# Tiles of x, of its sums and of the dense activations moved to 64 bytes off a multiple of 128

## The chip, the cores and the metric

One Trainium2 chip, one of its cores. The metric is device time in microseconds (us) of one launch. PE is TensorE, with PEld for its weight loads; DVE is VectorE, ACT ScalarE, POOL GpSimd, SP SyncE.

## What is computed

Three layers in a row on 1152 tokens of width 512, all in float32:

```python
scores = scale * q @ k.T + min(-(cum_i - cum_j), 0)   # causal, 2 x 8 heads, 576 x 64
x = softmax(scores) @ v                               # -> (1152, 512)
p = domain_probs / domain_probs.sum(-1)               # 4 experts
x = sum_e p[:, e] * (relu(x @ w1[e]) @ w2[e])         # w1 512 x 1024, w2 1024 x 512
out = (silu(x @ w_gate) * (x @ w_val)) @ w_out        # 512 x 1536, 1536 x 512
```

## The kernel before

A small planner inside the kernel (`Plan`) decides, with a table of costs and ranks, on which engine each step runs and in which order. It does so while the program is built, so the order on each engine is fixed then. The change touches none of its numbers.

**Exact products from parts.** Every operand of a dense matmul is held as a high part and a low part (`xh`/`xl` for x, `wah`/`wal`, `wsh`/`wsl` and `woh`/`wol` for weights, `hh`/`hl` for the activations between two matrices), and each product is three matmuls: high by high, high by low, low by high. Each matmul is one weight load of 128 by 128 (PEld) and one stream of 256, 320 or 512 columns (PE). The operand that streams is called moving here, the one that is loaded is called stationary.

**Into the hidden layer.** `into` (lines 1040 to 1042) does it plainly for the first five weights. After that `seven` (lines 1144 to 1146) does a block of 2 by 2 quarters with seven products instead of eight, from sums of quarters of the weight (`wsh`, `wsl`) and sums of quarters of x (tiles `xh0`, `xl0` for tokens 0 to 511, `xh512`, `xl512` for tokens 512 to 1151). In both, x or its sums are moving and the weight is stationary. The columns are 256 for the first half of the tokens and 320 for the second; one product is six matmuls. The table of the seven products, as (weight part, x part), says which tiles each one reads; a pair means the operand itself, a single number one of its sums:

```python
SEVEN = [((0, 0), (0, 0)), ((0, 1), (1, 0)), (0, 1), (2, 0), (1, 2), (3, (1, 1)), ((1, 1), 3)]
```

So products 0 and 1 read x itself with `wah`/`wal`; products 2, 3 and 4 read sums of x with `wsh`/`wsl`; product 5 reads x itself with `wsh`/`wsl`; product 6 reads sums of x with `wah`/`wal`. The trace leaves the numbers off tile names: `xh` there stands for `xh`, `xh0` and `xh512`, and the product tells which it is.

**Out of the hidden layer.** `outof` (lines 1202 to 1204): the activations `hh`, `hl` are stationary, the weights `woh`, `wol` are moving, 512 columns, three matmuls per block of 128 tokens and 128 hidden units. Results are taken from PSUM by DVE (line 1316, with the gate `pr`; line 1464 in the last layer).

**Order.** `merge` puts the `outof` work of one stage behind three quarters of the `seven` work of the next. A stage then reads: products 0 to 4 in one run of 30 matmuls, 3 matmuls of `outof`, product 5 (6 matmuls), some `outof`, product 6 (6 matmuls), the rest of `outof`.

**Where tiles lie.** A pool hands out its tiles one behind the other; each takes a multiple of 32 bytes of every partition. The pool `const` is at the bottom of SBUF, and the pool `tm` (opened when attention is done, line 1593) takes the space that attention leaves. The starts of the tiles, in bytes modulo 128, in the built programs:

| tiles | before | changed |
|---|---|---|
| `xh`, `xl` (x itself), `acc_a` | 0 | 64 |
| `xh0`, `xl0` (sums, first half) | 64 | 64 |
| `xh512`, `xl512` (sums, second half), `acc_b` | 0 | 64 |
| `hh`, `hl` in `tm`; also `cc`, `tt`, `x32`, `sg` | 0 | 64 |
| `hh`, `hl` in `hA` (first stages, and one weight in three of the last layer) | 0 | 0 |
| `wah`, `wal`, `wsh`, `wsl`, `woh`, `wol`, `raw`, `sf` | 0 | 0 |

All slices that a dense matmul reads start a multiple of 128 bytes into their tile, so the row of a tile holds for each of its matmuls. `xh0` and `xl0` lie at 64 before the change because the small tiles ahead of them in `const` (`pr` with 160 bytes, `warm` with 32) add up so.

Of the kernel before, what the change touches and what calls it, by code (L numbers as in the profile page):

```python
# [9 lines left out]
F32 = mybir.dt.float32  # L10
# [8 lines left out]
P = 128  # L19
# [3 lines left out]
HALF = 512  # L23
PIECES = 2
PLAIN = 5
NS = 5
NKQ = 8
NKP = 2
# [81 lines left out]
def dve(c, n=1):  # L110
    return n * 0.07 + 0.00105 * c
# [53 lines left out]
class Plan:  # L165
# [8 lines left out]
    def add(self, eng, cost, run=None, deps=(), take=(), give=(), rank=0.0, port="p", mode="r"):  # L174
        t = Task(eng, cost, run, [d for d in deps if d is not None], take, give, rank, port, mode)
        if not t.missing:
            self.ready.append(t)
        return t
# [102 lines left out]
def attention_moe_swiglu(ctx, tc, q_early, q_late, k, v, s, dp, w1, w2, wg, wv, wo, out):  # L281
# [4 lines left out]
    NT, _, DM = out.shape  # L286
    N = NT * P
    E = dp.shape[2]
# [15 lines left out]
    const = ctx.enter_context(tc.tile_pool(name="const", bufs=1))  # L304
# [2 lines left out]
    psw = ctx.enter_context(tc.tile_pool(name="psw", bufs=1, space=PSUM))  # L307

    ident = const.tile([P, P], F32, name="ident")
    xh = const.tile([P, NC, N], F32R, name="xh")  # L310
    xl = const.tile([P, NC, N], F32R, name="xl")
    acc_a = const.tile([P, HALF // P, DM], F32, name="acc_a")
    pr = const.tile([P, NT, E], F32, name="pr")
    late = {}
    plan = Plan()
    add = plan.add
    rings = {}
# [1 line left out]
    def ring(name, n=2):  # L319
        return rings.setdefault(name, Ring(n))  # L320
# [36 lines left out]
    def attention(ap, ps):  # L357
# [162 lines left out]
        def inorder(stage, t):  # L520
            before[stage] = t
            return t

        def group(i, pi, ch, qbs):
# [42 lines left out]
            def least(x, lane, at, w):  # L567
                def run():
                    if "st" not in box:
                        box["st"] = next(stats)  # L570
                    if lane not in box["ns"]:
                        box["ns"][lane] = ap.tile([P, S], F32, name="ns", tag="ns", bufs=NS)
                    st, ns = box["st"][:, 2 * x:2 * x + 2], box["ns"][lane]
                    if two:
                        todo = [(s0, s1, y[:, :s1 - s0], decay[pi, 2][:, s0:s1]) for y, (s0, s1) in zip(box["sp"], spans)]
                    else:
                        todo = [(at, at + w, box["sp"][lane][:, at:at + w], mask[:, 2 * P - w:] if pi < EXACT else decay[pi][:, lane, :w])]
                    for y, (s0, s1, sp, bias) in enumerate(todo):
                        nc.vector.tensor_tensor_reduce(
                            ns[:, s0:s1], sp, bias, SC, st[:, 0:1] if y else 3.0e38, op0=ALU.add, op1=ALU.min, accum_out=st[:, y:y + 1])  # L580
                return run
# [33 lines left out]
            for x, lane, (qb, at, w) in todo:  # L615
                new, final = lane not in owner, x == L - 1
                tM = inorder("m", add("dve", dve(w, len(spans)) + 0.01, least(x, lane, at, w), [tS if pi or lane else ready[-1], before.get("m")] + bias,
                                      take=[ring("ns", NS)] if new else [], give=[(tS, rg)] + (used[pi] if qbs[-1] == ch.qbs[-1] else [])
                                      if final else [], rank=i + x + RANK["m"]))
# [345 lines left out]
    narrow = [[Narrow(w[u]) for w in (wg, wv, wo)] for u in wide]  # L965
    halves_n = iter([(x, a) for u in narrow for x in u for a in range(2)])
    late["narrowed"] = []
    late["warm"] = const.tile([P, 1], F32, name="warm")
    w_in = [Weight(w1[i], False, "wa") for i in range(n1)]
    for w in w_in[PLAIN:]:  # L970
        w.plain = False
# [503 lines left out]
    def jobs():  # L1475
# [16 lines left out]
        late["pace"] = 2 * n1 - len(part) + sum(t1 < HALF for t1 in part) - CALM - REST  # L1492
        assert len(part) == PLAIN, len(part)
        for t0, t1 in ((0, HALF), (HALF, N)):
# [73 lines left out]
    def feed():  # L1568

        while sum(t.end is None for t in open_pe) < 6:  # L1570
            open_pe[:] = [t for t in open_pe if t.end is None]
            if not next(work, False):
                return
# [17 lines left out]
    with ExitStack() as st:  # L1591
        late["ps"] = st.enter_context(tc.tile_pool(name="psb", bufs=1, space=PSUM, reuse_waits="tile"))
        late["t"] = st.enter_context(tc.tile_pool(name="tm", bufs=2, reuse_waits="tile"))
        late["h"] = late["t"]
        late["acc"] = late["t"].tile([P, NT - HALF // P, DM], F32, name="acc_b", bufs=1)
        late["T", HALF] = {x: late["t"].tile([P, 4, 2, (N - HALF) // 2], F32R, name=f"x{x}{HALF}", bufs=1) for x in "hl"}
        sums_of_x(HALF)
        add("act", 1.3, lambda: nc.scalar.activation(late["warm"], late["warm"], AF.Silu), [late["gates"]], rank=0)
        late["made_n"] = 0
        plan.held, plan.ported = HELD2, False  # L1600
        rings["h"].n, rings["o"].n = 5, 3
        feed()
        while plan.step():
            feed()
# [70 lines left out]
```

## Time and profile before

| | us |
|---|---|
| median of 3 runs (697.23 to 697.93) | 697.86 |
| the profiled execution, its own time | 697.67 |
| its span, first to last instruction | 695.9 |
| PE busy in the span | 686.0 |
| DVE, POOL, ACT busy | 533.2, 461.8, 361.9 |

The span leaves 1.8 us of the execution's own time outside it. Rows of groups carry the busy time of one kind of instruction and its mean duration; matmuls are pipelined, so the duration of one (some 390 ns for 512 columns) is longer than its share of the engine. That share is the distance from the start of one matmul to the start of the next, which the rows in order of time show.

### The profile page before, as it was taken

Reading aid. Unit: us, or ns where it says so; the run is one execution under the profiler, and the core shown is the slowest. Engines: PE = TensorE matmul, PEld = TensorE weight load, DVE = VectorE, ACT = ScalarE, POOL = GpSimd, SP = SyncE. Lnnn points to the kernel's source line nnn. Section 1 sums busy time; section 2 is a strip of 40 time slices with the busy share of each in tenths; the row PEclk is TensorE's granted clock in tenths of the full one; section 3 lists DMA queues with packets and bytes.
Section 4 is the critical chain, followed back from the end, with each engine's and each line's share of the span. In section 5 each row is a group of like instructions: output and inputs, shape, how many; then the busy total and the mean of one; then the engine's idle time right before and its main releaser. Section 6 shows DMA issues by size and latency. Waiting matters only on the chain.

```text
span 695.9 us, 11938 instructions
## 1 busy us (share of the span) xinstructions
PE 686.0 (99%) x4267; PEld 600.4 (86%) x4267; DVE 533.2 (77%) x1086; ACT 361.9 (52%) x763; POOL 461.8 (66%) x464
## 2 busy tenths in 40 slices
PE   8999999999999999999999899999999999999998
PEld 6766667889898989898989799898999999999996
DVE  7866756795588999989988988786865766676665
ACT  7978777344655555554655654356555332323110
POOL 2888746786665776586667667598996838383211
PEclk9999999999999999999999999999999999999999
DMA  6786451120334455554653453213021111000003
GB/s 199 259 287 207 153 161 31 43 80 32 122 122 151 137 171 178 158 165 163 195 172 120 151 197 122 77 36 98 19 91 61 62 31 63 30 31 1 1 1 136
DMA packets 30187, 78.45 MB, mean 113 GB/s; under 512 B 3488, under 2 KB 8096, under 8 KB 30128
## 3 DMA queue, kind: packets, MB, share of 16 engines
q1 hardware_dynamic: 29984, 77.56, 34.2%
q8 instruction: 33, 0.54, 0.3%
q14 instruction: 26, 0.21, 0.1%
q10 hardware_dynamic: 144, 0.13, 0.1%
HBM read 65.85 MB, written 11.83 MB: 112 GB/s over the span
## 4 chain that ended last, share of the span: by engine, by line
PE 88%; DVE 4%; ACT 4%; DMA 2%; issue 1%; POOL 1%; SPq 0%; DVEq 0%; ACTq 0%; POOLq 0%
PE h L1146 13%; PE h L1145 13%; PE h L1144 13%; PE o L1202 13%; PE o L1203 12%; PE o L1204 12%; PE po L698 2%; PE tp L639 2%; ACT ns L588 2%; PE sp L557 2%; PE h L1040 1%; PE h L1042 1%; PE h L1041 1%; DMA d<-rows 1%; ACT ns L335 1%
## 5 line engine op out<-in xcount | busy, mean ns | idle before, releaser
L1163 DVE TENSOR_TENSOR cc<-cc,h 128x320 f32<-128x320 f32 (+1 forms) x306 | 137.0, 453 | 73.1 <-PE h L1146 62.0
L1202 PE MATMUL o<-woh,hh 128*128 128x512 f32 x398 | 157.6, 396 | 2.1 <-DVE xl L1355 1.1
L1203 PE MATMUL o<-wol,hh 128*128 128x512 f32 x398 | 155.6, 391 | 0.0
L1204 PE MATMUL o<-woh,hl 128*128 128x512 f32 x398 | 154.8, 389 | 0.0
L1144 PE MATMUL h<-xh,wsh 128*128 128x320 f32 (+1 forms) x344 | 101.7, 296 | 0.0
L1145 PE MATMUL h<-xl,wsh 128*128 128x320 f32 (+1 forms) x344 | 101.6, 295 | 0.0
L1146 PE MATMUL h<-xh,wsl 128*128 128x320 f32 (+1 forms) x344 | 101.6, 295 | 0.0
L1285 ACT ACTIVATE cc<-cc 128x640 f32<-128x640 f32 (+1 forms) x54 | 37.5, 695 | 104.3 <-DVE cc L1163 104.1
L340 POOL TENSOR_TENSOR wal<-raw,wah 128x512 fp32r<-128x512 f32 (+1 forms) x58 | 68.3, 1189 | 35.2 <-ACT wah L327 34.3
L1204 PEld LDWEIGHTS o<-woh,hl 128*128 128x128 f32 x398 | 74.8, 188 | 16.6 <-DVE hl L340 0.5
L1202 PEld LDWEIGHTS o<-woh,hh 128*128 128x128 f32 x398 | 74.8, 188 | 14.8 <-issue 1.3
L340 POOL TENSOR_TENSOR hl<-cc,hh 128x512 fp32r<-128x512 f32 (+1 forms) x28 | 41.9, 1495 | 68.1 <-ACT hh L1288 64.7
L340 POOL TENSOR_TENSOR wol<-raw,woh 128x512 fp32r<-128x512 f32 x54 | 75.8, 1419 | 13.2 <-ACT woh L327 12.4
L1203 PEld LDWEIGHTS o<-wol,hh 128*128 128x128 f32 x398 | 74.9, 188 | 9.9
L1146 PE MATMUL h<-xh,wal 128*128 128x320 f32 (+1 forms) x258 | 76.6, 297 | 0.0
L1145 PE MATMUL h<-xl,wah 128*128 128x320 f32 (+1 forms) x258 | 76.5, 297 | 0.0
L1144 PE MATMUL h<-xh,wah 128*128 128x320 f32 (+1 forms) x258 | 76.4, 296 | 0.0
L340 POOL TENSOR_TENSOR wsl<-sf,wsh 128x512 fp32r<-128x512 f32 x48 | 68.2, 1439 | 2.6 <-ACT wsh L327 2.5
L1144 PEld LDWEIGHTS h<-xh,wsh 128*128 128x128 f32 x344 | 64.7, 188 | 1.7
L1145 PEld LDWEIGHTS h<-xl,wsh 128*128 128x128 f32 x344 | 64.7, 188 | 1.6
L1146 PEld LDWEIGHTS h<-xh,wsl 128*128 128x128 f32 x344 | 64.7, 188 | 0.0
L1316 DVE SCALAR_TENSOR_TENSOR acc_b<-o,pr,acc_b 128x512 f32<-128x512 f32 x75 | 55.2, 742 | 5.6 <-PE o L1204 5.4
(158 smaller groups left out, 1557.4 us busy)
## 6 DMA issues: line engine op xcount, KB each, us to landing
raw<-in_w SPq DMA_DIRECT2D x42, 512.0 KB, 5.0
n<-hl SPq DMA_DIRECT2D x36, 256.0 KB, 2.4
raw<-n SPq DMA_DIRECT2D x18, 512.0 KB, 3.3
hh<-in_wg SPq DMA_DIRECT2D x12, 512.0 KB, 3.8
hh<-in_wv SPq DMA_DIRECT2D x12, 512.0 KB, 4.2
hh<-in_wo SPq DMA_DIRECT2D x12, 512.0 KB, 4.0
dql<-rows SPq DMA_DIRECT2D x8, 512.0 KB, 4.7
vr<-in_v SPq DMA_DIRECT2D x4, 640.0 KB, 4.5
```

What stands on the lines that cost most here:

```text
L340: {"v": nc.vector, "p": nc.gpsimd}[e].tensor_tensor(to, x, f32(y), op=ALU.subtract)
L557: nc.tensor.matmul(sp[j][:, at:at + w], Q[half[j], x], K[half[j], :w], start=True, stop=False)
L588: nc.scalar.activation(ns, ns, AF.Exp, bias=st[:, y:y + 1], scale=-1.0, accum_out=st[:, 8 + x:9 + x])
L1144: nc.tensor.matmul(hp, wh, h, start=c == 0, stop=False)
L1145: nc.tensor.matmul(hp, wh, l, start=False, stop=False)
L1146: nc.tensor.matmul(hp, wl, h, start=False, stop=c == 1)
L1163: nc.vector.tensor_tensor(part(k), part(x), banks[i], op=ALU.add)
L1202: nc.tensor.matmul(op, hh[:, f, ts], wh[:, f, y], start=f == 0, stop=False)
L1203: nc.tensor.matmul(op, hh[:, f, ts], wl[:, f, y], start=False, stop=False)
L1204: nc.tensor.matmul(op, hl[:, f, ts], wh[:, f, y], start=False, stop=f == NF - 1)
L1285: nc.scalar.activation(src()[:, o], src()[:, o], AF.Relu)
L1316: nc.vector.scalar_tensor_tensor(acc(t), bank_(), sc, acc(t), op0=ALU.mult, op1=ALU.add)
```

## The change

`pr` and `warm` are allocated ahead of `xh`, `xl` and `acc_a` instead of behind them, which moves those three by 192 bytes and leaves what follows where it was. In the pool `tm` a tile `line` of 64 bytes, which nothing reads or writes, comes first and moves every later tile of that pool by 64 bytes.

```diff
+LINE = 16
@@
     ident = const.tile([P, P], F32, name="ident")
+    pr = const.tile([P, NT, E], F32, name="pr")
+    late = {"warm": const.tile([P, 1], F32, name="warm")}
+
     xh = const.tile([P, NC, N], F32R, name="xh")
     xl = const.tile([P, NC, N], F32R, name="xl")
     acc_a = const.tile([P, HALF // P, DM], F32, name="acc_a")
-    pr = const.tile([P, NT, E], F32, name="pr")
-    late = {}
@@
-    late["warm"] = const.tile([P, 1], F32, name="warm")
@@
         late["h"] = late["t"]
+        late["t"].tile([P, LINE], F32, name="line", bufs=1)
         late["acc"] = late["t"].tile([P, NT - HALF // P, DM], F32, name="acc_b", bufs=1)
```

The lists of instructions of all engines are the same before and after, in the same order with the same shapes; only addresses differ.

## Rows read from the trace of the kernel before

**Rows 1.** Span and mean granted TensorE clock; then the page's busy time of the engines.
```profile
core 0: 695.9 us, clock 1.000
...
PE 686.0 (99%) x4267; PEld 600.4 (86%) x4267; DVE 533.2 (77%) x1086; ACT 361.9 (52%) x763; POOL 461.8 (66%) x464
```

**Rows 2.** The page: chain of work that ended last, by engine.
```profile
PE 88%; DVE 4%; ACT 4%; DMA 2%; issue 1%; POOL 1%; SPq 0%; DVEq 0%; ACTq 0%; POOLq 0%
```

**Rows 3.** Groups by shape, PE: first of the three lines of each product.
```profile
L1202 PE MATMUL o<-woh,hh 128*128 128x512 f32 x394 | 156.5, 397 | 2.1 <-DVE xl L1355 1.1 <-DVE acc_a L1316 1.0
...
L1144 PE MATMUL h<-xh,wsh 128*128 128x320 f32 x192 | 59.4, 309 | 0.0
...
L1144 PE MATMUL h<-xh,wah 128*128 128x320 f32 x144 | 44.4, 308 | 0.0
L1144 PE MATMUL h<-xh,wsh 128*128 128x256 f32 x152 | 42.4, 279 | 0.0
...
L1144 PE MATMUL h<-xh,wah 128*128 128x256 f32 x114 | 32.0, 281 | 0.0
L1040 PE MATMUL h<-xh,wah 128*128 128x256 f32 x48 | 14.0, 292 | 0.0
...
L1144 PE MATMUL h<-xh,hl 128*128 128x320 f32 x32 | 9.9, 308 | 0.0
...
L1144 PE MATMUL h<-xh,hh 128*128 128x320 f32 x24 | 7.4, 308 | 0.0
```

**Rows 4.** Order of time, PE, one stage of 256 columns: products 0 to 4.
```profile
296.26 0.28 PE L1146 MATMUL h<-xh,wal 128*128 128x256 f32 x1
...
297.46 0.29 PE L1144 MATMUL h<-xh,wsh 128*128 128x256 f32 x1
...
297.82 0.28 PE L1144 MATMUL h<-xh,wsh 128*128 128x256 f32 x1
...
299.52 0.39 PE L1202 MATMUL o<-woh,hh 128*128 128x512 f32 x1
```

**Rows 5.** The same stage: product 5, between two runs of `outof`.
```profile
299.75 0.40 PE L1203 MATMUL o<-wol,hh 128*128 128x512 f32 x1
299.99 0.39 PE L1204 MATMUL o<-woh,hl 128*128 128x512 f32 x1
300.22 0.28 PE L1144 MATMUL h<-xh,wsh 128*128 128x256 f32 x1
300.33 0.28 PE L1145 MATMUL h<-xl,wsh 128*128 128x256 f32 x1
...
300.93 0.40 PE L1202 MATMUL o<-woh,hh 128*128 128x512 f32 x1
```

**Rows 6.** Order of time, PE, a stage of 320 columns: products 2 to 4.
```profile
423.07 0.31 PE L1144 MATMUL h<-xh,wsh 128*128 128x320 f32 x1
...
425.71 0.39 PE L1202 MATMUL o<-woh,hh 128*128 128x512 f32 x1
```

**Rows 7.** Order of time, PE: a longer run of `outof`, 512 columns.
```profile
301.63 0.40 PE L1202 MATMUL o<-woh,hh 128*128 128x512 f32 x1
...
304.13 0.39 PE L1204 MATMUL o<-woh,hl 128*128 128x512 f32 x1
```

**Rows 8.** Order of time, PE: product 6 behind a run of `outof`.
```profile
305.04 0.28 PE L1144 MATMUL h<-xh,wah 128*128 128x256 f32 x1
...
305.74 0.39 PE L1202 MATMUL o<-woh,hh 128*128 128x512 f32 x1
```

**Rows 9.** Windows of 40 us: PE, PEld, DVE, ACT, POOL busy (count), clock, DMA, GB/s.
```profile
220.00:260.00 40.00, 40.00 (x235) 35.74 (x234) 37.43 (x60) 22.55 (x40) 28.78 (x23) 1.00 0.45 152
...
460.00:500.00 40.00, 39.95 (x254) 36.34 (x254) 30.73 (x57) 23.07 (x51) 37.80 (x41) 1.00 0.16 53
```

**Rows 10.** Groups by shape, ACT: casts of 256 columns.
```profile
L327 ACT CAST wah<-raw 128x256 fp32r<-128x256 f32 x19 | 7.7, 405 | 13.1 <-PE h L1145 12.9
...
L327 ACT CAST xh<-sf 128x256 fp32r<-128x256 f32 x7 | 2.8, 399 | 1.2 <-POOL sf L1082 1.2
```

## The prediction

> **What bounds the kernel now.** I read the page first: PE is busy 686.0 of 695.9 us at a granted clock of 1.000, and no other engine is above 77% [rows 1]. The chain that ended last agrees: 88% of it is PE [rows 2]. So the end is set by how fast PE gets through its list, above all in the dense part, from about 130 us on. There a busy share of 99% tells nothing, since matmuls overlap; I looked at the distance from start to start instead.
>
> At the granted clock of 1.00, the upper of the two levels (2.4 GHz), one column per cycle, 256, 320 and 512 columns need 106.7, 133.3 and 213.3 ns. The rows show more. A run of `outof` takes 2.50 us for 11 matmuls, 227.3 ns each [rows 7]: 14.0 over. The 18 matmuls of 320 columns take 2.64 us, 146.7 ns each [rows 6]: 13.4 over. So each matmul carries a surcharge that does not depend on its columns, as a cost of its weight load would.
>
> One stage of the kernel before holds the experiment already. Products 0 and 1 read x itself, at 0 modulo 128: the last ten of their twelve matmuls take 1.20 us, 120.0 ns each. Products 2 to 4 have the same shape and read the sums of x, which lie at 64: after three slower ones (0.36 us), the last fifteen take 1.70 us, 113.3 ns each [rows 4]. The stationary tile differs as well (`wah` there, `wsh` here), but product 5 tells these apart: it loads `wsh` and streams x itself, and from its second matmul on it takes 0.60 us for five, 120.0 ns each [rows 5]. So it goes with where the moving tile lies: 13.3 ns of surcharge with both operands at 0, 6.7 ns with 64 between them. The reading I take is that the stream and the weight load running beside it get in each other's way in SBUF, less so when they start in different halves of 128 bytes.
>
> The Trainium skill speaks against this reading: "TensorE: Matmul & The Clock Gate", Part 2, step 1, says that PE has two independent read ports into SBUF, so that loading the next weights takes no bandwidth from the running matmul. By that rule tile starts would not matter; the 120.0 beside 113.3 ns disagrees, and the rule gets a rival below.
>
> **The change, part by part.** No instruction is added, removed or moved. All costs come from addresses.
>
> *Streams that gain.* 320 columns: the groups have 192 + 144 per line, and two smaller ones (32 + 24) where the weight sits in `hA`, times three lines, 1176 matmuls [rows 3]. All of them go from 0/0 to 64/0. At 6.7 ns this is 7.9 us. 256 columns in `seven`: 152 + 114, and again 32 + 24, times three, 966; three products of seven read x itself, 414, and the rest lies at 64 already. With the 48 times three of `into` [rows 3] 558 gain: 3.7 us. 512 columns: 394 times three, 1182 [rows 3], less 84 early ones (counted in the program's list) whose activations lie in `hA` and stay at 0: 1098, at 6.7 ns 7.4 us. Here it is the stationary operand that moves. No row shows a stationary tile at 64 under a moving one at 0. Its price lies between nothing (only the moving start counts) and 6.7 ns (only the difference counts). I take 6.7, because the surcharge at 0/0 is nearly the same for all three lengths (13.3, 13.4, 14.0) and so looks like one cause with two equal partners. Together 19.0 us, the ceiling.
>
> *What switches take back.* PE changes between x and `outof` 131 times each way (counted in the list); most runs of x are of 6 or 30 matmuls, those of `outof` of 3 to 18. Around a switch the gain is not there. Product 6, six matmuls that already read at 64, takes 0.70 us behind `outof` [rows 8]; product 5, at 0, takes 0.71 [rows 5]. So six matmuls behind a switch gain about nothing, 40 ns a time. Some 110 of the 131 runs of x are among those counted above: 4.4 us. The first three of `outof` behind sums at 64 take 0.70 us, from 299.52 to 300.22 [rows 4, 5], against 0.68 in the steady run [rows 7]; I let them gain nothing either: 132 runs by 3 by 6.7 ns, 2.6 us. That leaves 12.0 us.
>
> A price of the skill's, for comparison: the same page, Part 1, gives a back-to-back matmul as its columns over the clock plus about 2.5 ns. Were that reached, the saving per matmul would be about 11 ns instead of 6.7, and the ceiling an estimated 31 us; the 113.3 ns at 64 show that this offset does not get there.
>
> *What reaches the end.* 12.0 us over some 560 us of dense work is 0.86 us in 40. The fullest neighbours are DVE, 37.43 of 40 us from 220 to 260, and POOL, 37.80 from 460 to 500 [rows 9]. Both have over 2 us left, more than 0.86. So neither becomes the bound, but queues get tighter and PE will meet a late operand more often. I take off a tenth: 10.8 us.
>
> *Other engines.* They read and write the moved tiles as well. The one clean pair is an ACT cast of 256 columns: 405 ns from 0 to 0, 399 ns into the sums at 64 [rows 10]. I put them at nothing: PE's work covers theirs as long as they keep the idle time of those windows [rows 9]. If DVE's operations became 2% longer, its fullest window would still fit in 40 us.
>
> **Sum.** 697.67 us of the profiled execution less 10.8 is 686.9; the median of the runs is 0.19 higher, so I forecast 687.1.
>
> **Rivals.**
> 1. *Nothing happens* (7%): the ports are independent and 113.3 comes from something else that goes with the sums, such as their being written by other engines. Against it stands product 5, which changes only the moving tile. Time 697.9.
> 2. *Only the moving start counts* (22%): the 512s keep 227 ns, since the weights stay at 0. For it: every row at 64 is one of a moving tile. The gain is (7.9 + 3.7 - 4.4) by 0.9, 6.5 us: 691.4.
> 3. *Only the 256s gain* (5%): at 320 and 512 columns the weight load ends well ahead of the stream, and the surcharge there has another cause. Against it: the equal surcharge. 3.7 us, less about half at switches: 696.0.
> 4. *No loss at switches* (10%): with all activations moved too, the pieces behind a switch settle at once; the whole ceiling reaches the end: 678.9.
> 5. *`outof` gets worse* (4%), the other side: a stationary tile at 64 under a stream from 0 does not settle, and each of the 1098 takes the 0.24 us that one matmul behind a switch shows, 299.75 to 299.99 [rows 5], instead of 0.227. That is 13 ns by 1098, 14 us, against the 6.5 us that x gains: 705.4. It decides from 6 ns more per matmul of `outof`, 233 ns, on.
>
> **How the numbers follow.** My own case has 52%; within it, losses at switches between none on `outof` and twice what I took put the time between 682 and 691. About 0.2%, 1.4 us, can be told from no change here. Faster by more than that: 52 + 22 + 5 + 10 = 89%. The same: 7%. Slower: 4%. The range leaves out rival 1, rival 5, rival 3 and about half of rival 4, some 20%: 680.0 to 695.0.
>
> **What would show it.** In the changed profile: products 0 and 1 at 256 columns at 113 ns from start to start in the run, 320 columns at 140, `outof` at 220 in its longer runs; six-long runs behind a switch near 0.70 us at 256 columns; the same durations on ACT and DVE; less idle time of DVE in the window from 220 us on. Wrong would be: 147 ns at 320 columns (rival 3 or 1), 227 at 512 (rival 2), over 233 (rival 5), or the spacings as forecast with new idle time on PE that keeps the end where it was (then my tenth was too little).

## The result and the profile after

The changed kernel takes 701.76 us (median of 4 runs, 701.03 to 701.91), the kernel before 697.89 beside it (4 runs). The ratio is 1.0053, with a 95% interval of 1.0035 to 1.0070: 3.9 us slower by the medians, where 10.8 us faster, 687.1, was forecast. The profiled execution has a span of 700.1 us, 4.2 more than [rows 1].

The page of the changed kernel, its engines:

```profile
span 700.1 us, 11938 instructions
...
PE 690.3 (99%) x4267; PEld 599.6 (86%) x4267; DVE 531.3 (76%) x1086; ACT 362.1 (52%) x763; POOL 462.0 (66%) x464
```

PE is busy 4.3 us longer, and DVE, ACT and POOL as long as before to within 2 us. So the time went into the matmuls themselves and not into waits, nor into more work of the other engines.

The changed kernel's groups by shape on PE (one of the three lines for 256 and 320 columns; lines lie one or two further down than before):

```profile
L1203 PE MATMUL o<-woh,hh 128*128 128x512 f32 x394 | 157.6, 400 | 2.1 <-DVE xl L1356 1.0 <-DVE acc_a L1317 1.0
L1205 PE MATMUL o<-woh,hl 128*128 128x512 f32 x394 | 155.8, 395 | 0.0
L1204 PE MATMUL o<-wol,hh 128*128 128x512 f32 x394 | 155.5, 395 | 0.0
L1145 PE MATMUL h<-xh,wsh 128*128 128x320 f32 x192 | 59.3, 309 | 0.0
...
L1145 PE MATMUL h<-xh,wah 128*128 128x256 f32 x114 | 31.8, 279 | 0.0
```

Beside [rows 3]: `outof` went from 397 to 400 ns on its first line, 320 columns stayed at 309, and the group of products 0, 1 and 6 at 256 columns fell from 281 to 279. The order of time shows what that is from start to start. PE, the same stage of 256 columns as [rows 4, 5, 7] (rows between those shown are left out):

```profile
298.54 0.28 PE L1145 MATMUL h<-xh,wah 128*128 128x256 f32 x1
...
301.27 0.39 PE L1203 MATMUL o<-woh,hh 128*128 128x512 f32 x1
...
301.96 0.28 PE L1145 MATMUL h<-xh,wsh 128*128 128x256 f32 x1
...
302.66 0.39 PE L1203 MATMUL o<-woh,hh 128*128 128x512 f32 x1
...
303.35 0.39 PE L1203 MATMUL o<-woh,hh 128*128 128x512 f32 x1
...
306.62 0.39 PE L1205 MATMUL o<-woh,hl 128*128 128x512 f32 x1
```

From 298.54 to 301.27 stand 24 matmuls, the last 6 of x itself and 18 of its sums, 113.8 ns each: here x itself goes as fast as its sums, where it took 120.0 ns in [rows 4]. Product 5 takes 0.70 us, as forecast. But the run of `outof` takes 3.27 us for 14 matmuls, 233.6 ns each, against 227.3 in [rows 7]. And a run of 320 columns has not moved: 18 matmuls in 2.64 us, 146.7 ns each, as in [rows 6].

```profile
425.58 0.31 PE L1145 MATMUL h<-xh,wsh 128*128 128x320 f32 x1
...
428.22 0.39 PE L1203 MATMUL o<-woh,hh 128*128 128x512 f32 x1
```

The surcharge of a matmul is the time from its start to the next start, less its columns at the granted 2.4 GHz. Added up over all dense matmuls of each trace (the 2% of gaps with over 40 ns of surcharge are left out):

| surcharge | matmuls | before, us (mean ns) | changed, us (mean ns) |
|---|---|---|---|
| `outof`, 512 columns | 1136 | 17.7 (15.6) | 22.1 (19.5) |
| x itself, 256 columns | 545 | 6.7 (12.3) | 5.4 (9.8) |
| sums of x, 256 columns | 548 | 4.7 (8.7) | 5.1 (9.4) |
| 320 columns | 1171 | 15.3 (13.1) | 15.4 (13.1) |
| all, with some 50 others | | 45.3 | 48.8 |

That is 3.5 of the 4.2 us. The "others" are mainly matmuls of `into` with 512 columns, which stream x and which the prediction did not count: they too got slower, from 16.0 to 20.0 ns. The missing 0.7 us is there by 37 us into the matmuls, in attention, before most dense work; its cause is not shown, and it may be the spread of single executions (696.5 to 700.9 for the kernel before in later comparisons).

### The profile page after: what moved, and what is told of

Read it like the earlier page. It is cut to its first block, busy times and chain, and to the rows that moved or that the text cites. A ratio compares the mean times of both kernels' runs of the same rounds, so it can differ in the third digit from the quotient of the medians.

```text
span 700.1 us, 11938 instructions
## 1 busy us (share of the span) xinstructions
PE 690.3 (99%) x4267; PEld 599.6 (86%) x4267; DVE 531.3 (76%) x1086; ACT 362.1 (52%) x763; POOL 462.0 (66%) x464
## 4 chain that ended last, share of the span: by engine, by line
PE 83%; DVE 4%; POOL 4%; ACT 3%; DMA 3%; issue 2%; SPq 1%; POOLq 0%; ACTq 0%; DVEq 0%
PE h L1145 13%; PE h L1146 13%; PE h L1147 13%; PE o L1203 12%; PE o L1205 12%; PE o L1204 12%; ACT ns L590 2%; PE po L700 1%; DMA d<-rows 1%; PE tp L641 1%; POOL sf L1083 1%; PE h L1041 1%; PE h L1043 1%; PE h L1042 1%; DMA raw<-in_w 1%
## 5 line engine op out<-in xcount | busy, mean ns | idle before, releaser
L1205 PE MATMUL o<-woh,hl 128*128 128x512 f32 x398 | 156.9, 394 | 0.0
L342 POOL TENSOR_TENSOR wol<-raw,woh 128x512 fp32r<-128x512 f32 x54 | 75.8, 1419 | 13.5 <-ACT woh L329 12.7
```

Source lines behind the costliest of these rows:

```text
L342: {"v": nc.vector, "p": nc.gpsimd}[e].tensor_tensor(to, x, f32(y), op=ALU.subtract)
L1205: nc.tensor.matmul(op, hl[:, f, ts], wh[:, f, y], start=False, stop=f == NF - 1)
```

## The experiments

Twelve kernels were run. The first four, timed together, take the change apart and move other tiles instead. "Distance" is the start of the stationary tile less that of the moving one; starts are those of the built programs.

**x alone.** The first half of the change's diff (`pr` and `warm` ahead of `xh`) without `line`.

> Only x itself and acc_a move to 64; sums of the second half and the activations stay at 0. If the loss of the change comes from outof alone, products that read x itself at 256 columns go from 120 ns to 113 to 117 ns, 320 columns stay at 147, outof at 227, and the time falls by 558 x 3 ns, 1.6 us, to 696.3. If moving x is what costs (rival: later data for PE, other engines slower on moved tiles), the time is 698 to 702.

It took 698.19 us, ratio 0.9998 (0.9986 to 1.0011): no difference. The trace tells why. x itself gains 1.2 us (12.3 to 10.2 ns on the mean), but the sums, which nobody moved, lose 1.2 us (8.7 to 10.8 ns). Products 0 to 4 now run in one steady state, and it is not the 113 ns of before: all eleven runs of 30 settle at 117.8 ns. Groups on PE: first line of `outof`, then products 2 to 5 (mostly sums, 279 ns before) and products 0, 1 and 6 (mostly x itself, 282 ns before on this line):

```profile
L1201 PE MATMUL o<-woh,hh 128*128 128x512 f32 x394 | 156.1, 396 | 2.1 <-DVE xl L1354 1.1 <-DVE acc_a L1315 1.0
...
L1143 PE MATMUL h<-xh,wsh 128*128 128x256 f32 x152 | 42.7, 281 | 0.0
...
L1144 PE MATMUL h<-xl,wah 128*128 128x256 f32 x114 | 32.0, 281 | 0.0
```

So a pair of starts does not have one price: the sums lie where they did and take longer behind x at 64 than behind x at 0. `outof` stays at 15.4 ns, so its loss belongs to the second half of the change.

**Weights of `outof` alone at 64**, then **weights and activations at 64**.

```diff
+                first = self.tag == "wo" and "line_w" not in late
+                if first:
+                    late["line_w"] = wp.tile([P, 16], F32, name="line_w", bufs=1)
                 parts = [wp.tile([P, W], F32R, name=self.tag + x, tag=self.tag + x, bufs=2) for x in "hl"]
+                if first:
+                    wp.tile([P, 16], F32, name="line_v", bufs=1)
@@ the second kernel only, behind xh512 and xl512
+        late["t"].tile([P, 16], F32, name="line2", bufs=1)
```

> x and activations as before, only woh and wol (the streams of outof) at 64. Theory D, the difference of the two starts decides: outof goes from 227 to 233 ns as in the changed kernel, 1182 x 3.9 ns on the mean, 4.6 us, 702.5. Theory S, only the start of the stationary tile decides: outof stays at 227, 697.9.

> woh, wol and the activations hh, hl all at 64, x as before. Theory D: no difference between the starts, outof back at 227 ns, 697.9 (the 84 early matmuls of outof alone are at 64 over 0). Theory S: the stationary tile at 64 costs 6 ns, outof at 233, 702.

The first took 701.38 us, ratio 1.0039 (1.0026 to 1.0052); the second 701.03, 1.0037 (1.0023 to 1.0051). `outof` has a surcharge of 19.2 and 19.1 ns. The first result speaks for theory D and against S. The second speaks against D: with both tiles at 64 modulo 128 the loss should be gone by D; S, which forecast it, had failed at the first. The two paddings, 128 bytes together, had also moved everything behind them by 128, the activations among it. Modulo 256 the distances in `outof` are therefore 64 in the first kernel and 128 in the second. That was the hint that 128 is not the period.

**Sums of the first half at 0 too**, with 64 bytes ahead of `xh0` and 64 behind `xl0`.

> The sums of the first half, at 64 before by accident, are put at 0 as well, so that every dense operand starts at 0. If the 113 ns come from the 64 bytes, products 2 to 4 at 256 columns go to 120 ns, 552 x 3.7 ns on the mean, 2.0 us slower, 699.9. If they come from something else that goes with the sums, they stay at 113 and the time at 697.9.

It took 700.73 us, ratio 1.0035 (1.0022 to 1.0047): the sums go from 8.7 to 12.7 ns, 2.3 us, and `outof`, whose distance stayed at 0, from 15.6 to 16.4. The 113 ns of before did come from the accident in the layout. (Here the weights moved by 128 against x, so for x and these sums it is the distance 128 and not 0.)

**Matmuls alone.** A kernel that has only PE at work, in blocks of 24 matmuls, tells whether other engines or the order matter. Its tiles a, b, c and d start at 0, 32, 64 and 96 bytes; the blocks of 320 and 512 columns are alike.

```python
OFF = {"a": 0, "b": 32, "c": 64, "d": 96}
REPS = 24
...
    def block256(m, s):
        for i in range(REPS):
            nc.tensor.matmul(bank[turn[0] % 4][:, :256], stat[s][:, i % 8 * P:i % 8 * P + P], move[m][:, i % 4 * 256:i % 4 * 256 + 256], start=True, stop=True)
            turn[0] += 1
```

> Only matmuls, no other engine at work: blocks of 24 matmuls of 256, 320 and 512 columns, moving and stationary tiles at 0, 32, 64 and 96 in all 16 pairs, forward and then backward; the kernel leaves the rest of the computation out. Theory D (the difference of the starts decides): at each length the spacing is the same for equal differences; 120 at 0 and 113 at 64 for 256 columns, and 227 at equal starts for 512. Theory H (what decides is a phase that is left by the matmuls before, and the starts only shift it): the same pair has another spacing in the backward pass. Theory N (neighbours: other engines reading SBUF make the surcharge): all pairs are alike and at the columns over the clock plus 3 ns.

Groups by shape of that kernel; `mva` to `mvd` are moving tiles, `sta` to `std` stationary ones:

```profile
L48 PE MATMUL pp<-mva,stc 128*128 128x512 f32 x48 | 11.5, 396 | 0.0
...
L48 PE MATMUL pp<-mvc,sta 128*128 128x512 f32 x48 | 11.3, 392 | 0.0
...
L48 PE MATMUL pp<-mvb,stb 128*128 128x512 f32 x48 | 11.2, 389 | 0.0
...
L43 PE MATMUL pp<-mva,sta 128*128 128x320 f32 x48 | 7.4, 309 | 0.0
...
L43 PE MATMUL pp<-mva,stc 128*128 128x320 f32 x48 | 7.4, 308 | 0.0
...
L38 PE MATMUL pp<-mvb,stb 128*128 128x256 f32 x48 | 6.1, 283 | 0.0
...
L38 PE MATMUL pp<-mva,stc 128*128 128x256 f32 x48 | 5.9, 279 | 0.0
```

Theory N falls: nothing else runs, and the surcharges are there. Equal starts give 120.0, 146.7 and 226.7 ns in the settled part of each block (its second half; start to start, at 512 columns some 162 ns less than the durations shown), whatever came before. At 320 columns every pair settles near 146.7. At 512, the stationary tile at 64 over a stream from 0 gives 233.3 and the reverse 228.9. Pairs of equal distance agree within 0.4 ns at 512 columns, as theory D has it. So equal starts are the best case at 512 columns, among the worst at 256, and no matter at 320. Theory H holds at 256: the pair 0 and 64 settled at 117.8 in one pass and at 113.3 in the other.

**The order of a stage alone.** The same, with the runs of a stage: 30 of x, 3 of `outof`, 6, 15, 6, 6.

> The order of matmuls of a stage (30 of x, 3 of outof, 6 of x, 15 of outof, 6 of x, 6 of outof) and nothing else, for x, its weight, the weight of outof and the activations each at 0 or 64, with 256 and with 320 columns; the rest of the computation is left out. If the surcharge of 6 ns per matmul of outof in the changed kernel comes from PE's own reads, outof takes 227 ns with everything at 0 and 233 with the activations at 64, here too, and a stage with x and activations at 64 is longer by about 0.07 us at 320 columns (24 x 4 ns less nothing) than one with all at 0. If it comes from other engines on the moved tiles, all stages of one length are alike within 0.02 us.

PE, 320 columns; the second of two stages with everything at 0, then the second with the activations at 64 (names that end in `c`), each from the first to the start of the next:

```profile
382.54 0.30 PE L38 MATMUL pp<-xha,wha 128*128 128x320 f32 x1
...
394.20 0.30 PE L38 MATMUL pp<-xha,wha 128*128 128x320 f32 x1
...
405.71 0.40 PE L40 MATMUL pp<-oha,hlc 128*128 128x512 f32 x1
405.94 0.30 PE L38 MATMUL pp<-xha,wha 128*128 128x320 f32 x1
...
417.70 0.30 PE L38 MATMUL pp<-xha,wha 128*128 128x320 f32 x1
```

11.66 us against 11.76: 0.10 us for 24 matmuls of `outof`, 4 ns each, as in the whole kernel (15.6 to 19.5). With x at 64 as well it was 11.76. So the loss of the change is PE's own, with no other engine in it. At 256 columns the stages lie between 10.25 us (x and weights of `outof` at 64, the rest at 0) and 10.64.

**The period.** One moving tile, the stationary one 0 to 960 bytes further on.

> As the kernel with matmuls alone, with the moving tile at one place and the stationary one 0, 64, 128, ... 960 bytes further on (modulo 1024), forward and backward; the rest of the computation is left out. Theory P128 (what counts is the distance modulo 128): 0, 128, 256, ... are alike, 227 ns at 512 columns, and 64, 192, 320, ... are alike, 233 ns. Theory P256 (modulo 256): 128 is not like 0 at 512 columns (more than 227), 256 is; 64 gives 233 and 192 gives 229, as +64 and -64 did. If neither, the period shows in the list.

The groups at 512 columns, `sta` at 0, `stb` at 64, and so on in steps of 64:

```profile
L48 PE MATMUL pp<-mva,stf 128*128 128x512 f32 x48 | 11.5, 395 | 0.0
L48 PE MATMUL pp<-mva,stb 128*128 128x512 f32 x48 | 11.5, 395 | 0.0
...
L48 PE MATMUL pp<-mva,stc 128*128 128x512 f32 x48 | 11.5, 395 | 0.0
L48 PE MATMUL pp<-mva,stg 128*128 128x512 f32 x48 | 11.5, 395 | 0.0
...
L48 PE MATMUL pp<-mva,std 128*128 128x512 f32 x48 | 11.3, 392 | 0.0
L48 PE MATMUL pp<-mva,sth 128*128 128x512 f32 x48 | 11.3, 392 | 0.0
...
L48 PE MATMUL pp<-mva,ste 128*128 128x512 f32 x48 | 11.2, 389 | 0.0
L48 PE MATMUL pp<-mva,sti 128*128 128x512 f32 x48 | 11.2, 389 | 0.0
```

The period is 256 bytes: `stb` and `stf` are alike, `stc` and `stg`, `std` and `sth`, and `ste` and `sti`. From start to start, in the settled part of each block, forward and backward:

| stationary less moving, modulo 256 | 256 columns | 320 | 512 |
|---|---|---|---|
| 0 | 120.0, 120.0 | 146.7 | 226.7 |
| 64 | 117.8, 113.3 | 146.7 | 233.3 |
| 128 | 118.2, 118.3 | 146.7 | 231.7, 232.6 |
| 192 | 117.8, 113.3 | 146.7 | 228.9 |

Theory P256 holds. At 128 the spacing does not stand still but goes round, 115 to 122 ns at 256 columns and 228 to 241 at 512; the two figures there, and 119.1 in one pass at 896, differ by where such a round is cut. At 960, with 256 columns, both passes settled at 117.8.

**Two tests of that table in the whole kernel.** The activations by 128 in the kernel before, and `line` with 192 bytes in the changed one:

```diff
@@ the kernel before, behind xh512 and xl512
+        late["t"].tile([P, 32], F32, name="line2", bufs=1)
@@ the changed kernel
-        late["t"].tile([P, LINE], F32, name="line", bufs=1)
+        late["t"].tile([P, 48], F32, name="line", bufs=1)
```

> The kernel before with the activations (and cc, tt, x32, sg) 128 bytes further on, so that every dense tile but the sums of the first half stays at a multiple of 128. Theory P128: nothing changes, outof at 227 ns, 697.9. Theory P256: outof leaves its 227 ns, about 3 ns more on the mean as in the kernel with weights and activations at 64, where the distance was 128 as well: 1098 x 3 ns, 701.

> The changed kernel with a line of 192 bytes instead of 64, so that the activations lie 64 bytes below the weights of outof modulo 256 instead of above; modulo 128 nothing differs. Theory P128: as the change, outof at 233, 701.8. Theory P256: outof at 229 in runs, 4 ns less than in the change, 1098 x 4 ns, 697.5.

The first took 701.55 us, ratio 1.0055 (1.0039 to 1.0072): modulo 128 nothing was moved, and it lost as much as the change. The second took 697.64, ratio 0.9993 (0.9980 to 1.0006): modulo 128 it is the change, and the loss is gone. Both as P256 says. In the second, `outof` keeps a small part of its loss (16.4 ns, 15.6 before), and x itself (8.5 ns) and its sums (7.8) pay for it. First line of `outof`, with the activations at 128 and with the line of 192:

```profile
L1202 PE MATMUL o<-woh,hh 128*128 128x512 f32 x394 | 157.9, 401 | 2.1 <-DVE xl L1355 1.0 <-DVE acc_a L1316 1.0
```

```profile
L1201 PE MATMUL o<-woh,hh 128*128 128x512 f32 x394 | 156.2, 397 | 2.2 <-DVE xl L1354 1.0 <-DVE acc_a L1315 1.0
```

**The activations alone**, the second half of the change in its smallest form (`line2` of 64 bytes in the kernel before), and **two layouts after the table**: activations at distance 192, sums of the second half at 0, x at 64 or at 192 from its weights.

> Only the second half of the change: activations (and cc, tt, x32, sg) 64 bytes further on, x and its sums as before. If the activations alone make the loss, outof takes 233 ns in runs, 1098 x 3.9 ns on the mean, 4.3 us, 702. Rival (the loss needs x at 64 too, at the switches): outof at about 230, 699.

> x itself at 64 as in the change, sums of the second half at the distance 0 of before, activations 192 bytes further on, so 192 from the weights of outof modulo 256. By the matmuls alone: outof 229 ns in runs, 256 columns at 113 with this pair of distances, 320 unchanged: as with the line of 192 bytes, 44 us of surcharge in all instead of 45.3, 697. Rival (only distance 0 is worth having for outof): 699.

> As the one before, but x itself and the sums of the first half 64 bytes above their weights instead of below (distance 192 instead of 64 modulo 256). With matmuls alone this pair settled at 113.3 ns for all of x (10.25 us a stage against 10.33 to 10.45): 696.5. If the side does not matter in the kernel, 697.

The activations alone: 701.89 us, ratio 1.0054 (1.0041 to 1.0066), `outof` at 19.6 ns. That is the whole loss. First line of `outof`:

```profile
L1202 PE MATMUL o<-woh,hh 128*128 128x512 f32 x394 | 158.0, 401 | 2.1 <-DVE xl L1355 1.0 <-DVE acc_a L1316 1.0
```

x at 64: 697.44, ratio 1.0002 (0.9988 to 1.0016); the surcharges of its one trace add up to 43.7 us against 45.3, but the measured time shows no gain. x at 192: 699.84, ratio 1.0026 (1.0016 to 1.0037), a miss: all of x settled at 11 ns of surcharge, 117.8 ns from start to start, where the forecast had taken 113.3, the better of the two states that the table has for that distance; `outof` was at 16.7. No layout that was tried is faster than the kernel before beyond the interval.

Two kernels differ in nothing but the place of the activations (and of `cc`, `tt`, `x32`, `sg`): x alone at 64, with `outof` at the distance 0, and x at 64 with `outof` at 192. Yet x changes its pace too. 18 matmuls from the middle of the same run of products 0 to 4, first x alone, then x at 64 with the activations at 192:

```profile
297.86 0.28 PE L1143 MATMUL h<-xh,wah 128*128 128x256 f32 x1
...
299.98 0.28 PE L1143 MATMUL h<-xh,wsh 128*128 128x256 f32 x1
```

```profile
297.33 0.28 PE L1143 MATMUL h<-xh,wah 128*128 128x256 f32 x1
...
299.37 0.28 PE L1143 MATMUL h<-xh,wsh 128*128 128x256 f32 x1
```

That is 2.12 us against 2.04, 117.8 ns against 113.3. Of the eleven runs of 30, all settle at 117.8 in the first kernel and ten at 113.3 in the second; in the change nine are at 113.3 and two at 117.8. So where the tiles of the `outof` matmuls lie helps to decide at which pace the run of x behind them settles.

## Why the prediction was wrong

**What bounds the kernel** was right. PE's spacing sets the time, the surcharge is PE's own, and a few ns on 1100 matmuls moved the end by about what they add up to.

**x itself at 256 columns** was right in kind and mis-sized: 113.8 ns in the run shown, but 1.4 us in all instead of 3.7 less switches, and the sums lost 0.4 of it. The prediction gave the distance 64 one price; the runs show two, 113.3 and 117.8 ns.

**The step that failed** is the one from 256 columns to the other lengths: "the surcharge at 0/0 is nearly the same for all three lengths (13.3, 13.4, 14.0) and so looks like one cause with two equal partners". The equality is real, since matmuls alone at equal starts have 13.3 ns over the columns at each length (the 14.0 of [rows 7] is that with a slower start of the run). But equal surcharges at one distance said nothing on how each length takes another distance. At 320 columns none helps; the term of 7.9 us was 0. At 512 the distance 0 is the best there is, and the term of 7.4 us gained was 4.4 us lost. The sentence before it named the gap, that no row shows a stationary tile at 64 under a stream from 0, and then bounded its price by nothing and 6.7 ns gained. A loss had to be in those bounds: nothing in the trace excluded it, and the fifth rival had found a price for one, the 0.24 us of an `outof` matmul behind a switch [rows 5]. What the sum took back at switches and for the tenth came in the main off gains that were not there.

**The reading of halves of 128 bytes** failed as well. It is the distance modulo 256, with a sign: 64 and 192 are alike modulo 128 in size and cost 233.3 and 228.9 ns. The kernel before could not show that, since it has the distances 0 and 64 alone.

**The rivals.** The fifth, `outof` gets worse, came true where it was given 4%; its price of 13 ns was too high (6.6 with matmuls alone, 4.0 on the mean in the kernel), and the matmuls did settle, only at a slower pace. The third was right that 320 and 512 columns gain nothing, but it had no loss at 512; its reason, a weight load that ends early, no run tests. The rule of the Trainium skill behind the first ("TensorE: Matmul & The Clock Gate", Part 2, step 1, two independent read ports) says that loading weights takes nothing from the running matmul. These runs do not bear out what the prediction drew from it, that starts would not matter: with PE alone at work, the distance of the two starts by itself moves a matmul of 512 columns between 226.7 and 233.3 ns. Whether the two reads meet in SBUF is not shown.

**Switches, other engines.** Product 5 behind a switch took 0.70 us, as forecast. No other engine became the bound, and the busy time of none rose by more than 0.2 us, though single groups that touch moved tiles went either way.

What goes on inside SBUF or PE at a distance of 64 was not shown, only where and how much. How one and the same pair comes to settle in one state or another at 256 columns is also left open: the runs show only that it depends on the matmuls before.

## What to carry to other kernels

Where PE runs back to back, as here, the distance between the starts of the streaming and the loaded tile modulo 256 is a knob of 3% per matmul at 512 columns (226.7 to 233.3 ns) and 6% at 256 (113.3 to 120.0). With matmuls alone its best value was 0 for 512 and 64 or 192 for 256, and at 320 it did nothing. So measure each length by itself, in a kernel of matmuls alone, before moving a tile that several lengths share; then measure in the real kernel too, since at 256 columns the matmuls ahead of a run decided between 113.3 and 117.8. A small tile put anywhere ahead of others moves all of them: look at the addresses of every operand of the hot matmuls before and after an edit, whatever the edit was for.

## What the runs showed that was not expected

- The period is 256 bytes, not 128: with the activations moved by 128 the kernel took 701.55 us beside 698.38 (ratio 1.0055).
- The settled spacing depends on the matmuls before. At 256 columns one pair of starts settles at 113.3 or at 117.8 ns, moving x alone changed the surcharge of its unmoved sums from 8.7 to 10.8 ns, and moving the activations alone changed that of x. At the distance 128 the eleven runs of 30 settled at 120.0 ns in the whole kernel, where the table has 118.2.
- At 320 columns all 16 pairs, and all 16 distances, settle near 146.7 ns, 13.3 over the columns; only the first few matmuls of a block differ.
